# Attention and a two-layer MLP on one core: lower weight parts by subtraction, products kept back at two block changes, the last tile evicted in halves

## The chip, the cores and the metric

The kernel runs on one core of a Trainium2 chip. The engines are TensorE (PE, with its weight loads shown as PEld), VectorE (DVE), ScalarE (ACT), GpSimd (POOL) and SyncE (SP, which here only issues transfers). Matmuls write to PSUM; VectorE and ScalarE read PSUM and write SBUF; transfers (DMA) move data between HBM and SBUF, or within SBUF. The metric is the device time of one execution in microseconds (us), as the median over several runs.

## The reference

Linear attention over 8 batches of 576 tokens (8 heads of 64), then an MLP over all 4608 tokens, in float32:

```python
q_s = softmax(q, axis=-1);  k_s = softmax(k, axis=sequence)
kv = einsum('bhsd,bhse->bhde', k_s, v)
x  = einsum('bhsd,bhde->bhse', q_s, kv)        # as rows: 4608 x 512
h  = x @ w_in                                   # 512 x 2048
g  = h * clip(h + 3, 0, 6) / 6
out = g @ w_out                                 # 2048 x 512
```

The weights arrive as float64; the kernel gets their raw words and makes float32 values of them on the chip.

## The kernel before

**Accuracy.** A float32 matmul is made of three passes in the type float32r: each factor is split into a high part (a cast, ScalarE) and a low part (value minus high part, VectorE), and high x high, high x low and low x high are added up in PSUM. `split` (L121) does a cast and a subtraction; many lines call it, so L123 (the cast) and L124 (the subtraction) stand for many places, told apart by tile names.

**Blocks.** The 4608 rows are NB = 9 blocks `j` of 512 rows. d_ff is NFC = 16 chunks `f` of 128. For each chunk the first GEMM (`gemm1`, tile `ph`, 12 matmuls of 128x512) makes h, the activation makes `g` with its two parts, and the second GEMM (`gemm2`, 4 tiles `po` of 128x512, one PSUM bank each, 12 matmuls) adds the chunk's product into the block's output. Of a chunk's 12 passes, four use the lower part of w_out. After chunk 15, `store` (L596) evicts the four `po` tiles, times 1/6, into `ob` tiles (tile 0 and 2 by ScalarE at L606, 1 and 3 by VectorE at L604) and sends each by SP's queue (L607). `ob` has two buffers, except in the last block.

**Decoding.** In block 0, `decode(f)` (L136) turns a chunk of w_in and w_out (both sides of `raw`, 128x1024 words) into `v` and then into high and low parts in the tile `w_f`: `wi[f]` for w_in, `wo[f]` for w_out. For chunks 0 to 9 that is a split. For chunks 10 to 15 the low part is made in two steps: ScalarE writes -v, rounded to float32r (L168), and a transfer issued by GpSimd adds v to it in place (L169, 512 KB). `v` has three buffers, shared with other tiles (`m` in L306 and L457, `ts`, `xs`).

**Blocks 2 to 8** use a Strassen-like scheme for two chunks (a pair) at once: `fast_pair` (L498) makes seven products of six matmuls of 128x256 each, into `x`, `y` (tile `ph`) and `z` (tile `pz`); ScalarE and VectorE combine them into `first` and `second`, and from those `g` and its two parts, which are put in the space of wi[12], wi[13] for even pairs and wi[14], wi[15] for odd ones (`places`, L520). The factors from the weights are prepared once for each pair by `fast_weights` (L451): three quarters of the pair's w_in (A11, A12, A22) are stored to HBM as they are (L456), four sums S1 to S4 are formed on VectorE (L459 to L470, in `m` and two `ob` tiles), split into the space of that pair's own w_in, and stored (L473, two stores). `fetch` (L486) brings them back, through a ring of 12 places in wi[6] to wi[11] (L495). The factors from x are made by `x_factors`.

**The order.** Python traces the program, and a planner (a list scheduler that simulates the engines) lays out each engine's and each queue's instructions by readiness, traced order and marked priority; each engine and queue then keeps that order. From block 1 on (`in_order`, L684) TensorE keeps the order as traced. The second GEMM lags: its matmuls wait in the list `pend`, from which they are taken by `fill_one` (a whole chunk) or `fill(n)` (n matmuls). In block 0, up to two chunks are kept back; block 1 starts with `gemm1(1, 0)`, then both of them, and each chunk's second GEMM follows one chunk later. In blocks 2 to 8 `fast_pair` calls `slot(n)` between its products to put in 4, 7, 7 and 6 matmuls of the pair before. `slot` also advances `step`, the attention of the next block (L310), whose loads, softmax and small matmuls run beside the MLP. `fast_weights` of pairs 0 to 6 is called in block 1 after each odd chunk, that of pair 7 in block 2's first pair, in its fourth slot.

Of the kernel before, what the change touches and what calls it, by code (L numbers as in the profile page):

```python
# [10 lines left out]
F32 = mybir.dt.float32  # L11
# [7 lines left out]
P = 128  # L19
# [11 lines left out]
def attention_moe(  # L31
# [89 lines left out]
    def split(hi, lo, src, engine=nc.vector):  # L121

        nc.scalar.copy(hi, src)  # L123
        engine.tensor_sub(lo, src, hi.bitcast(F32))  # L124
# [11 lines left out]
    def decode(f):  # L136

        n = 2 * DM
        pairs = raws.pop(f).rearrange("p (n two) -> p n two", two=2)
        low, high = pairs[:, :, 0], pairs[:, :, 1]
        v = moe.tile([P, n], F32, name="v", bufs=3)
        m = v
        nc.scalar.activation(m, high.bitcast(F32), AF.Abs)
        nc.vector.tensor_scalar(m, m, W_MIN, W_MAX, op0=ALU.max, op1=ALU.min)  # L149
        m = m.bitcast(U32)  # L150
        nc.vector.tensor_scalar(
            m, m, 3, 0x3FFFFFFF, op0=ALU.logical_shift_left, op1=ALU.bitwise_and
        )
        vu = v.bitcast(U32)
        nc.vector.scalar_tensor_tensor(  # L155
            vu, high, 0xC0000000, m, op0=ALU.bitwise_and, op1=ALU.bitwise_or
        )
        nc.scalar.activation(low, low, AF.Copy, scale=2.0**-29)
        nc.vector.tensor_tensor(vu, vu, low, op=ALU.add)  # L159
        parts = place(f, F32R, f"w_{f}").rearrange("p (s i n) -> p s i n", s=2, i=2)  # L160
        vs = v.rearrange("p (s n) -> p s n", s=2)
        if f < 10:
            split(parts[:, :, 0], parts[:, :, 1], vs)
        else:

            hi, lo = parts[:, :, 0], parts[:, :, 1]
            nc.scalar.copy(hi, vs)
            nc.scalar.mul(lo, vs, -1.0)  # L168
            nc.gpsimd.dma_start(lo.bitcast(F32), vs, accum_op=ALU.add)  # L169
        wi[f], wo[f] = parts[:, 0], parts[:, 1]  # L170

    FAST = 2
# [277 lines left out]

    def fast_weights(pair):  # L451

        a, b = wi[2 * pair], wi[2 * pair + 1]
        kept[pair] = d = dr.tile([P, 7, 2, HT], F32, name=f"wf{pair}")
        for n, src in ((A11, a[:, :, 0:HT]), (A12, a[:, :, HT:]), (A22, b[:, :, HT:])):
            nc.sync.dma_start(d[:, n], src.bitcast(F32))  # L456
        whole = moe.tile([P, 2 * DM], F32, name="m", tag="v", bufs=3)  # L457
        for at, src in ((0, a), (TB, b)):
            nc.vector.tensor_add(  # L459
                whole[:, at : at + TB], src[:, 0].bitcast(F32), src[:, 1].bitcast(F32)  # L460
            )
        a11, a12, a21, a22 = (whole[:, n * HT : (n + 1) * HT] for n in range(4))
        hi, lo = (t.rearrange("p e n -> p (e n)") for t in (a, b))
        s12, s34 = (moe.tile([P, DM], F32, name="ob", bufs=2) for _ in range(2))
        s1, s2, s3, s4 = (t[:, n : n + HT] for t in (s12, s34) for n in (0, HT))
        nc.vector.tensor_add(s1, a21, a22)
        nc.vector.tensor_sub(s2, s1, a11)
        split(hi[:, 0:TB], lo[:, 0:TB], s12)
        nc.vector.tensor_sub(s3, a11, a21)
        nc.vector.tensor_sub(s4, a12, s2)  # L470
        split(hi[:, TB:], lo[:, TB:], s34)
        for e, t in enumerate((hi, lo)):
            nc.sync.dma_start(  # L473
                d[:, S1 : S4 + 1, e], t.bitcast(F32).rearrange("p (k n) -> p k n", k=4)
            )
# [22 lines left out]
    def fast_pair(j, pair, fill):  # L498

        to = factors(j)  # L500
        x = ps_h.tile([P, TB], F32, name="ph", tag="ph")[:, 0:HT]
        y = ps_h.tile([P, TB], F32, name="ph", tag="ph")[:, 0:HT]
        z = ps_a.tile([P, TB], F32, name="pz", tag="pa")[:, 0:HT]
        seen = set()

        def product(n, ps, name):
            w_hi, w_lo = (come[j, pair, n][:, e] for e in (0, 1))
            f_hi, f_lo = (to[ORDER[n][1]][:, e] for e in (0, 1))
            for i in range(2):
                c = slice(i * P, (i + 1) * P)  # L510
                for k, (w, f) in enumerate(((w_hi, f_hi), (w_hi, f_lo), (w_lo, f_hi))):
                    first = name not in seen
                    seen.add(name)
                    mm(ps, w[:, c], f[:, i], first, i == 1 and k == 2, True)
            del come[j, pair, n]
            fetch(1)

        first = moe.tile([P, TB], F32, name="first", tag="g_hi", bufs=3)
        second = moe.tile([P, TB], F32, name="second", tag="g_lo", bufs=3)
        places = [wi[12 + 2 * (pair % 2) + n] for n in (0, 1)]  # L520
        product(0, z, "z")
        product(1, x, "x")
        with tc.high_priority():
            nc.scalar.copy(first[:, 0:HT], x)
        fill(4)
        product(2, y, "y")
        nc.vector.tensor_add(first[:, 0:HT], first[:, 0:HT], z)
        product(3, x, "x")
        with tc.high_priority():
            nc.scalar.copy(second[:, 0:HT], x)  # L530
        fill(7)
        product(4, x, "x")
        with tc.high_priority():
            nc.scalar.copy(second[:, HT:], x)  # L534
            nc.vector.tensor_add(second[:, HT:], second[:, HT:], y)  # L535
        fill(7)
        product(5, x, "x")
        r = moe.tile([P, TB], F32, name="g", bufs=2)
        with tc.high_priority():
            nc.scalar.activation(r[:, HT:], x, AF.Relu, bias=three, scale=1.0)  # L540
            nc.vector.scalar_tensor_tensor(  # L541
                r[:, HT:], r[:, HT:], 6.0, x, op0=ALU.min, op1=ALU.mult
            )
        h = first[:, 0:HT]
        nc.scalar.activation(r[:, 0:HT], h, AF.Relu, bias=three, scale=1.0)
        nc.vector.scalar_tensor_tensor(
            r[:, 0:HT], r[:, 0:HT], 6.0, h, op0=ALU.min, op1=ALU.mult
        )
        gs = [(places[0][:, 0], places[0][:, 1])]
        split(*gs[0], r)  # L550
        fill(6)
        product(6, y, "y")
        with tc.high_priority():
            nc.vector.tensor_add(second[:, 0:HT], second[:, 0:HT], y)  # L554
        r = moe.tile([P, TB], F32, name="g", bufs=2)
        nc.scalar.activation(r, second, AF.Relu, bias=three, scale=1.0)  # L556
        nc.vector.scalar_tensor_tensor(r, r, 6.0, second, op0=ALU.min, op1=ALU.mult)  # L557
        gs.append((places[1][:, 0], places[1][:, 1]))
        split(*gs[1], r)
        return gs  # L560
# [35 lines left out]
    def store(j, po):  # L596
        for t in range(NTT):
            if j < NB - 1:
                ob = moe.tile([P, DM], F32, name="ob", bufs=2)
            else:  # L600
                ob = place(t, F32, f"ob{t}")[:, 0:DM]
            with tc.high_priority():
                if t % 2:
                    nc.vector.tensor_scalar_mul(ob, po[t], 1.0 / 6.0)  # L604
                else:
                    nc.scalar.mul(ob, po[t], 1.0 / 6.0)  # L606
            nc.sync.dma_start(out[j * TB + t * P : j * TB + (t + 1) * P, :], ob)  # L607


    nc.scalar.activation(three, three, AF.Exp)  # L610
# [67 lines left out]
    for j in range(FAST):  # L678
        for f in range(NFC):
            if j == 0:  # L680
                if f + AHEAD < NFC:
                    load_w(f + AHEAD)
            elif not in_order:
                in_order.append(True)  # L684
            g = gemm1(j, f)
            if j == 0:
                if f + 2 < NFC:
                    decode(f + 2)
            elif f % 2:
                if f < 15:  # L690
                    fast_weights(f // 2)
                if f >= 7:
                    fetch(1 if f < 15 else 12 - len(come))
            next(step, None)

            while len(pend) > 1 - j:
                fill_one()
            pend.append(work(j, [f], [g]))
    for j in range(FAST, NB):
        for pair in range(NFC // 2):  # L700
            done = [0]

            def slot(n):
                fill(n)
                done[0] += 1
                if done[0] in (2, 4):
                    next(step, None)
                if j == FAST and not pair and done[0] == 4:
                    fast_weights(NFC // 2 - 1)

            gs = fast_pair(j, pair, slot)
            fill()
            pend.append(work(j, [2 * pair, 2 * pair + 1], gs))
# [60 lines left out]
```

## Time and profile before

| what | value |
|---|---|
| time, median of 3 runs | 892.21 us (889.02 to 894.39) |
| the profiled execution's own time | 890.79 us |
| its span, first to last instruction | 888.9 us |
| busy share of the span: PE, PEld, DVE, ACT, POOL | 97%, 83%, 69%, 52%, 15% |
| mean granted TensorE clock | 0.99 |
| block 0's first `gemm1` | 33.27 us |
| block 1's first `gemm1` | 137.23 us |
| block 2's first product | 244.00 us |
| TensorE's last matmuls / last eviction | 881.87 us (12, 3.31 us) / 885.20 us |
| mean HBM rate | 204 GB/s |

Times of the trace are microseconds from the span's start. In the views of groups a row gives line, engine, operation, output and inputs, shapes, count, then busy time and the mean duration of one in ns, then the idle time of the engine just before them and what ended it. In the view of waits a row gives who waited for whom: total in us, times, the longest. In the chain of waits and the timeline a row gives start, length and what ran; a bracket gives the idle time before it and what ended that. Matmuls overlap in these rows, so the length of one (about 0.39 us) is more than its spacing (12 in 2.78 us). SPq is SP's queue of transfers; "to landing" is from issue to the last byte.

### The profile page before, as it was taken

To read this page: it belongs to the slowest core of one execution; us is meant where nothing else is said; L and a number is where in the kernel's file an instruction comes from. 1 tells how busy PE (TensorE), PEld (TensorE's weight loads), DVE (VectorE), ACT (ScalarE), POOL (GpSimd) and SP (SyncE) were. 2 spreads that over 40 slices of the span, in tenths; PEclk is the share of its full clock that TensorE was granted. 3 is DMA by queue.
4 is the path that set the end of the run, shared out by engine and by line. 5 is a ranking of instruction groups with operands and counts; after the bars stand their busy time and mean duration, and the time that the engine had idled before them with its cause. 6 is when DMAs were issued, how large, how long until landed. Compare 5 with 4: busy or idle time off the path is not lost.

```text
span 888.9 us, 15262 instructions
## 1 busy us (share of the span) xinstructions
PE 858.4 (97%) x5380; PEld 739.2 (83%) x5380; DVE 614.6 (69%) x1266; ACT 464.8 (52%) x944; POOL 132.9 (15%) x329
## 2 busy tenths in 40 slices
PE   5799998999999999999999999999999999999998
PEld 3578776787789888888888888888888888889896
DVE  7999867899777766767585757676867565444333
ACT  7998753544445454545454545444554554434333
POOL 5000132021212110202020202021212120100000
PEclk9899999999999999999999999999999999999999
DMA  9992583538487668676777668676755575567541
GB/s 372 413 369 84 125 203 136 180 108 289 161 259 224 219 202 258 216 224 203 228 233 229 209 220 259 200 230 195 256 158 183 161 230 170 167 178 224 170 140 47
DMA packets 98474, 185.19 MB, mean 208 GB/s; under 512 B 9824, under 2 KB 24160, under 8 KB 96352
## 3 DMA queue, kind: packets, MB, share of 16 engines
q1 hardware_dynamic: 96192, 180.03, 62.3%
q0 software_dynamic: 1632, 3.15, 2.0%
q10 hardware_dynamic: 576, 1.05, 0.3%
q8 instruction: 43, 0.70, 0.3%
q14 instruction: 31, 0.25, 0.1%
HBM read 156.93 MB, written 24.12 MB: 204 GB/s over the span
## 4 chain that ended last, share of the span: by engine, by line
PE 83%; DVE 7%; DMA 6%; ACT 2%; issue 1%; POOL 0%; SPq 0%; ACTq 0%; DVEq 0%; POOLq 0%
PE po L91 41%; PE ph L91 33%; PE pz L91 4%; PE px L91 2%; PE pkv L91 2%; DMA w<-v 2%; DMA qt<-in_qf_dram 2%; DVE w L124 1%; DMA out_dram<-ob 1%; DVE v L155 1%; DVE v L149 0%; DMA wf<-w 0%; POOL swap L289 0%; DVE km L267 0%; DVE v L159 0%
## 5 line engine op out<-in xcount | busy, mean ns | idle before, releaser
L91 PE MATMUL po<-w,w 128*128 128x512 f32 x1008 | 260.8, 394 | 0.8 <-ACT w L123 0.8
L91 PEld LDWEIGHTS po<-w,w 128*128 128x128 f32 x1008 | 178.4, 189 | 30.7 <-ACT w L123 1.1
L91 PE MATMUL ph<-x_lo,w 128*128 128x256 f32 (+1 forms) x800 | 152.2, 305 | 2.7 <-DVE x_lo L124 2.3
L91 PEld LDWEIGHTS ph<-w,w 128*128 128x128 f32 x1008 | 133.8, 190 | 11.0 <-DVE second L535 1.4
L91 PE MATMUL ph<-x_hi,w 128*128 128x256 f32 (+1 forms) x592 | 138.4, 338 | 4.4 <-DMA w<-v 3.3
L91 PE MATMUL ph<-w,w 128*128 128x256 f32 x1008 | 140.4, 284 | 1.2 <-DVE second L535 1.2
L91 PEld LDWEIGHTS ph<-x_lo,w 128*128 128x128 f32 x800 | 117.0, 189 | 17.0 <-DVE x_lo L124 2.6
L91 PEld LDWEIGHTS ph<-x_hi,w 128*128 128x128 f32 x592 | 93.3, 191 | 18.8 <-DMA w<-v 3.5
L124 DVE TENSOR_TENSOR w<-g,w 128x512 fp32r<-128x512 f32 x112 | 77.2, 689 | 35.3 <-ACT w L123 35.3
L123 ACT CAST w<-g 128x512 fp32r<-128x512 f32 x112 | 69.4, 619 | 56.7 <-DVE g L541 34.4
L91 PE MATMUL po<-w 128*128 128x512 f32 x336 | 86.7, 394 | 0.1
L91 PEld LDWEIGHTS po<-w 128*128 128x128 f32 x336 | 59.4, 188 | 10.8 <-ACT w L123 0.5
L91 PE MATMUL po<-w,g_hi 128*128 128x512 f32 x256 | 67.4, 401 | 0.9 <-ACT g_hi L123 0.9
L556 ACT ACTIVATE g<-second,three 128x512 f32<-128x512 f32 x56 | 40.5, 724 | 33.9 <-DVE second L554 26.5
L91 PEld LDWEIGHTS po<-w,g_hi 128*128 128x128 f32 x256 | 47.7, 190 | 12.2 <-ACT g_hi L123 1.4
L540 ACT ACTIVATE g<-ph,three 128x256 f32<-128x256 f32 x56 | 26.6, 474 | 57.9 <-PE ph L91 57.9
L541 DVE SCALAR_TENSOR_TENSOR g<-g,ph 128x256 f32<-128x256 f32 x56 | 23.2, 415 | 47.1 <-ACT g L540 47.0
L534 ACT COPY second<-ph 128x256 f32<-128x256 f32 x56 | 20.8, 372 | 63.1 <-PE ph L91 63.1
L557 DVE SCALAR_TENSOR_TENSOR g<-g,second 128x512 f32<-128x512 f32 x56 | 39.0, 697 | 15.3 <-ACT g L556 15.2
L91 PE MATMUL pz<-x_hi,w 128*128 128x256 f32 x336 | 49.5, 283 | 0.0
L535 DVE TENSOR_TENSOR second<-second,ph 128x256 f32<-128x256 f32 x56 | 23.1, 413 | 37.5 <-ACT second L534 37.5
L289 POOL COPY swap<-qr 32x16 f32<-32x16 f32 x112 | 30.6, 273 | 96.4 <-DVE qr L301 92.8
(125 smaller groups left out, 1264.2 us busy)
## 6 DMA issues: line engine op xcount, KB each, us to landing
w<-wf SPq DMA_DIRECT2D x392, 256.0 KB, 3.0
raw<-in_w_dram SPq DMA_DIRECT2D x16, 1024.0 KB, 13.4
out_dram<-ob SPq DMA_DIRECT2D x36, 256.0 KB, 3.3
vt<-in_v_dram SPq DMA_DIRECT2D x28, 325.0 KB, 3.5
wf<-w SPq DMA_DIRECT2D x16, 512.0 KB, 4.7
kt<-in_kT_dram SPq DMA_DIRECT2D x28, 288.0 KB, 3.0
ke<-in_k_dram SPq DMA_DIRECT2D x24, 320.0 KB, 2.9
qt<-in_qf_dram SPq DMA_DIRECT2D x28, 256.0 KB, 3.0
```

The costliest lines, as they stand in the source:

```text
L91: nc.tensor.matmul(out, lhsT, rhs, start=start, stop=stop, skip_group_check=goes_on)
L123: nc.scalar.copy(hi, src)
L124: engine.tensor_sub(lo, src, hi.bitcast(F32))
L155: nc.vector.scalar_tensor_tensor(vu, high, 0xC0000000, m, op0=ALU.bitwise_and, op1=ALU.bitwise_or)
L289: nc.gpsimd.tensor_copy(swap[r : r + QD], stat[o : o + QD])
L534: nc.scalar.copy(second[:, HT:], x)
L535: nc.vector.tensor_add(second[:, HT:], second[:, HT:], y)
L540: nc.scalar.activation(r[:, HT:], x, AF.Relu, bias=three, scale=1.0)
L541: nc.vector.scalar_tensor_tensor(r[:, HT:], r[:, HT:], 6.0, x, op0=ALU.min, op1=ALU.mult)
L556: nc.scalar.activation(r, second, AF.Relu, bias=three, scale=1.0)
L557: nc.vector.scalar_tensor_tensor(r, r, 6.0, second, op0=ALU.min, op1=ALU.mult)
```

## The change

1. `decode`, chunks 10 to 15: the lower part of w_in is now made by a VectorE subtraction (128x512); only that of w_out is still negated by ScalarE and completed by the adding transfer (128x512, 256 KB). Chunks 0 to 9 stay as they were.
2. Block 0 to 1: `fill_one()` runs the second GEMM of chunk 14 of block 0 ahead of block 1's first `gemm1`; chunk 15's stays behind it.
3. Block 1 to 2: at block 1's last chunk, the second GEMM of chunk 14 is kept back too, so 24 matmuls instead of 12 go into block 2's first pair. `fast_pair` calls its fill function with 0 there, which `slot` turns into 4 matmuls ahead of the first product, without advancing the attention.
4. `fast_weights` of pair 7 is called in block 1 after chunk 15, like the other pairs, and writes its sums into wi[12] and wi[13] (pair 6's space), since wi[14] and wi[15] are just in use.
5. The last tile of the last block is evicted in two halves: columns 256 to 511 by VectorE, sent by SP's queue; columns 0 to 255 by ScalarE, sent by ScalarE's queue; neither is marked for priority.

```diff
         vs = v.rearrange("p (s n) -> p s n", s=2)
-        if f < 10:
-            split(parts[:, :, 0], parts[:, :, 1], vs)
+        hi, lo = parts[:, :, 0], parts[:, :, 1]
+        nc.scalar.copy(hi, vs)
+        if f < BY_DMA:
+            nc.vector.tensor_sub(lo, vs, hi.bitcast(F32))
         else:
 
-            hi, lo = parts[:, :, 0], parts[:, :, 1]
-            nc.scalar.copy(hi, vs)
-            nc.scalar.mul(lo, vs, -1.0)
-            nc.gpsimd.dma_start(lo.bitcast(F32), vs, accum_op=ALU.add)
+            nc.vector.tensor_sub(lo[:, 0], vs[:, 0], hi[:, 0].bitcast(F32))
+            nc.scalar.mul(lo[:, 1], vs[:, 1], -1.0)
+            nc.gpsimd.dma_start(lo[:, 1].bitcast(F32), vs[:, 1], accum_op=ALU.add)
         wi[f], wo[f] = parts[:, 0], parts[:, 1]
...
         a11, a12, a21, a22 = (whole[:, n * HT : (n + 1) * HT] for n in range(4))
-        hi, lo = (t.rearrange("p e n -> p (e n)") for t in (a, b))
+        at = 2 * min(pair, NFC // 2 - 2)
+        hi, lo = (wi[at + n].rearrange("p e n -> p (e n)") for n in (0, 1))
...
         places = [wi[12 + 2 * (pair % 2) + n] for n in (0, 1)]
+        if (j, pair) == (FAST, 0):
+            fill(0)
         product(0, z, "z")
...
+            rows = out[j * TB + t * P : j * TB + (t + 1) * P, :]
+            if (j, t) == (NB - 1, NTT - 1):
+
+                a, b = slice(0, DM // 2), slice(DM // 2, DM)
+                nc.vector.tensor_scalar_mul(ob[:, b], po[t][:, b], 1.0 / 6.0)
+                nc.scalar.mul(ob[:, a], po[t][:, a], 1.0 / 6.0)
+                nc.sync.dma_start(rows[:, b], ob[:, b])
+                nc.scalar.dma_start(rows[:, a], ob[:, a])
+                continue
             with tc.high_priority():
...
-            nc.sync.dma_start(out[j * TB + t * P : j * TB + (t + 1) * P, :], ob)
+            nc.sync.dma_start(rows, ob)
...
             elif not in_order:
                 in_order.append(True)
+
+                fill_one()
             g = gemm1(j, f)
...
             elif f % 2:
-                if f < 15:
-                    fast_weights(f // 2)
+                fast_weights(f // 2)
                 if f >= 7:
                     fetch(1 if f < 15 else 12 - len(come))
             next(step, None)
 
-            while len(pend) > 1 - j:
+            while len(pend) > (1 if j == 0 or f == NFC - 1 else 0):
                 fill_one()
...
             def slot(n):
-                fill(n)
+                fill(n or 4)
+                if not n:
+                    return
                 done[0] += 1
                 if done[0] in (2, 4):
                     next(step, None)
-                if j == FAST and not pair and done[0] == 4:
-                    fast_weights(NFC // 2 - 1)
```

## The prediction

> **What bounds the kernel now.** I read the page first, then TensorE's waits from 60 to 260 us, then busy time by stretch (columns: stretch and length; busy time and count of PE, PEld, DVE, ACT, POOL; granted clock, DMA share, GB/s).
>
> ```profile
> span 888.9 us, 15262 instructions
> ...
> PE ph L91 <- DMA w<-v: 3.3, 2, 3.0
> PE ph L91 <- DVE x_lo L124: 2.3, 1, 2.3
> PE ph L91 <- DVE second L535: 1.2, 1, 1.2
> PE ph L91 <- ACT x_hi L123: 0.7, 1, 0.7
> PE po L91 <- ACT g_hi L123: 0.5, 1, 0.5
> PE ph L91 <- ACT second L534: 0.4, 1, 0.4
> ...
> 60.00:95.00 35.00, 35.00 (x172) 28.11 (x172) 33.95 (x50) 30.32 (x67) 1.34 (x1) 1.00 0.42 125
> 95.00:145.00 50.00, 43.80 (x219) 33.72 (x218) 39.57 (x71) 27.99 (x44) 12.79 (x26) 0.97 0.68 170
> 145.00:244.00 99.00, 98.46 (x511) 78.62 (x510) 82.59 (x175) 45.47 (x84) 18.93 (x49) 1.00 0.53 175
> 262.00:878.00 616.00, 614.94 (x4113) 547.91 (x4113) 387.56 (x850) 296.24 (x633) 86.77 (x229) 1.00 0.65 204
> ...
> 113.00:117.00 4.00, 3.88 (x12) 3.14 (x13) 1.55 (x3) 2.12 (x3) 2.87 (x5) 0.71 0.82 223
> 117.00:120.00 3.00, 3.00 (x11) 2.19 (x11) 2.57 (x5) 2.80 (x5) 0.25 (x1) 0.82 0.57 98
> 254.00:258.00 4.00, 4.00 (x20) 3.90 (x21) 3.45 (x9) 1.91 (x4) 1.77 (x5) 0.57 0.81 216
> ```
>
> From 262 to 878 us TensorE has 1 us idle in 616: nothing can be won there but by fewer matmuls, and the change takes none away. What it can win lies between 60 and 260 us: six waits of 8.4 us together, and a slower clock behind two of them, 4 us x (1 - 0.71) + 3 us x (1 - 0.82) = 1.7 us after the first, 4 us x (1 - 0.57) = 1.7 us after the last. (I count lost clock only where a stretch shows it.) The rows also show what a gain must live with: VectorE is 97% busy up to 95 us, 79% to 145 us, 83% to 244 us.
>
> The Trainium skill (TensorE: Matmul & The Clock Gate, "The HAM clock gate") says that the clock falls after at least one idle window of about 3.4 us. By that rule gaps as short as these would cost no clock and the sum below would be 3.4 us smaller; the trace disagrees, with 0.71 and 0.57 after shorter gaps, so the rows are used.
>
> **Lower parts of w_in without a transfer.** Six chunks (10 to 15) are decoded with the transfer.
>
> ```profile
> 106.71 6.36 DMA w<-v
> ...
> 113.12 0.73 PE L91 MATMUL ph<-x_hi,w 128*128 128x512 f32 x2 [2.96 <-DMA w<-v]
> 124.32 2.02 PE L91 MATMUL po<-w,g_hi 128*128 128x512 f32 x8
> 133.66 0.73 PE L91 MATMUL ph<-x_hi,w 128*128 128x512 f32 x2 [0.30 <-DMA w<-v]
> ...
> SPq L456 <- DMA w<-v: 31.5, 6, 7.7
> ...
> L124 DVE TENSOR_TENSOR w<-g,w 128x512 fp32r<-128x512 f32 x112 | 77.2, 689 | 35.3 <-ACT w L123 35.3
> L168 ACT ACTIVATE w<-v 128x1024 fp32r<-128x1024 f32 x6 | 6.4, 1060 | 0.0
> ```
>
> Chunk 12's transfer is issued at 106.71 and lands 6.36 us later; the first GEMM waits 2.96 us for it, and 0.30 us for chunk 15's. Now that lower part comes from one 128x512 VectorE subtraction (0.689 us, the nearest form), done some 1 to 2 us after the cast, so before 109 us. Removed: 2.96 + 0.30 us and the 1.7 us of clock, **-5.0 us**. ScalarE saves half of each 1.06 us negation, 3.2 us in all, which buys nothing by itself. The transfer halves to 256 KB and now gates only w_out: chunk 12's second product runs at 124.32 us, 11 us after even the old landing, so its price is nothing; that cover gone, it would be the old 3 us. SP's queue stood 31.5 us behind those transfers before its L456 stores, with the loads of k and q of the next blocks queued behind it; half of that wait (the stores of A11, A12, A22 take only w_in) goes.
>
> Added: 6 x 0.689 = 4.1 us of VectorE, five of the six after 95 us: 3.4 us. It runs beside TensorE, yet VectorE is what is next late. The stretch from 95 to 145 us would shrink to about 42.2 us (50 - 5.0 - 2.8, the next part) and hold 39.57 + 3.4 = 43.0 us of VectorE. At the 97% packing of the row before it that needs 44.3 us, so 2.1 us of the gain are lost if no VectorE work can slide; some can, since fast_weights of pair 0 and softmax of block 2 already stand in this stretch. Bounds 0 to 2.1; I take **+1.0 us**.
>
> **A product kept back between blocks 0 and 1.**
>
> ```profile
> 133.64 1.29 DVE L459 TENSOR_TENSOR m<-w 128x512 f32<-128x512 f32 x2 [1.99 <-DMA w<-v]
> ...
> 140.92 0.50 PE L91 MATMUL ph<-x_hi,w 128*128 128x512 f32 x1 [0.68 <-ACT x_hi L123]
> 143.69 0.51 PE L91 MATMUL ph<-x_lo,w 128*128 128x512 f32 x1 [2.27 <-DVE x_lo L124]
> ...
> 152.90 2.78 PE po L91 x12
> ```
>
> Block 1's first GEMM starts before its last head's x is split and waits 0.68 + 2.27 us, while 24 matmuls of block 0 stand behind it. fill_one() puts 12 of them in front: 2.78 us of cover. x_lo itself also comes earlier by up to the 1.99 us for which VectorE stood behind a transfer. What the x chain loses by the new subtractions is in the 1.0 us above. Bounds: nothing won (x_lo is later by as much) to 2.95; I take **-2.8 us**.
>
> **Products kept back into block 2, and pair 7 prepared one block earlier.**
>
> ```profile
> 252.56 0.69 DVE L604 TENSOR_SCALAR ob<-po 128x512 f32<-128x512 f32 x1 [1.62 <-DMA out_dram<-ob]
> 253.96 1.17 PE L91 MATMUL ph<-w,w 128*128 128x256 f32 x6 [1.24 <-DVE second L535]
> 255.21 0.62 ACT L123 CAST w<-g 128x512 fp32r<-128x512 f32 x1 [1.97 <-DVE g L541]
> ...
> 232.57 0.37 SPq L473 DMA_DIRECT2D wf<-w  x1
> ...
> 263.14 0.62 SPq L473 DMA_DIRECT2D wf<-w  x1
> ...
> L459 DVE TENSOR_TENSOR m<-w 128x512 f32<-128x512 f32 x16 | 10.2, 672 | 2.0 <-DMA w<-v 2.0
> L124 DVE TENSOR_TENSOR w<-ob,w 128x512 fp32r<-128x512 f32 x16 | 10.5, 683 | 4.1 <-PE ph L91 4.1
> L554 DVE TENSOR_TENSOR second<-second,ph 128x256 f32<-128x256 f32 x56 | 23.3, 416 | 4.7 <-PE ph L91 4.3
> ...
> wf<-w SPq DMA_DIRECT2D x16, 512.0 KB, 4.7
> ```
>
> In the first pair of block 2 VectorE stands 1.62 us behind an output transfer with `second` queued after it, and TensorE waits 0.44 + 1.24 us and then runs at 0.57. Only 12 matmuls of block 1 lie between that pair's products now; with 24 (4, 4, 7, 7 and 2) it has the filling of every later pair, and the row from 262 us shows no waits with that filling. Block 1's eviction also moves behind product 5. I take the whole wait and its clock: 0.44 + 1.24 + 1.7, **-3.4 us**; bounds 0 (the stall stands at the eviction's new place) to 3.4. The 0.5 us wait for g_hi stays.
>
> fast_weights of pair 7 moves as a whole: on VectorE 2 x 0.672 + 4 x 0.416 (another 128x256 sum, L554, stands for L466 to L470) + 2 x 0.683 = 4.4 us, two casts on ScalarE, and five stores on SP. They go out of the crowded first pair into 145 to 244 us, where VectorE has 16.4 us idle: no price. That cover gone it would be up to 4.4 us. Its new scratch is chunks 12 and 13, which pair 6's last store (232.57 us, landing 4.7 us later in the median, 237.3) must have left. The first pair of block 2 then puts its g there (the cast at 255.21 us): 18 us for 1.4 us of splits and a 4.7 us store, so nothing is charged; the late case is a rival below.
>
> **The last tile.**
>
> ```profile
> 885.20 0.69 DVE ob L604
> ...
> L534 ACT COPY second<-ph 128x256 f32<-128x256 f32 x56 | 20.8, 372 | 63.1 <-PE ph L91 63.1
> ...
> DMA to landing us min/median/max: 2.0/2.0/2.1
> ...
> w<-wf SPq DMA_DIRECT2D x392, 256.0 KB, 3.0
> ...
> ke<-in_k_dram SPq DMA_DIRECT2D x24, 320.0 KB, 2.9
> ```
>
> One 0.69 us eviction becomes a VectorE half (L554's 0.416) and a ScalarE half (0.372). Side by side that saves 0.28 us; one after the other it costs 0.10 us. No row shows two engines reading one PSUM tile without a dependence between them; I take **0**. A half's transfer, 128 KB, has no row: by size alone it would land 1.0 us sooner than the tail's 2.0; but loads of 320 KB land as soon as those of 256 (2.9 and 3.0), and 512 KB take 4.7, so between nothing and all I take nothing, nearest the loads; bounds 0 to -1.0.
>
> The Trainium skill (PSUM — Partial Sum Buffer, "PSUM bank collisions raise a hardware error") speaks against the halves: two engines may not touch one bank in the same partitions at once, and the compiler adds a dependency. By that rule the halves run in turn and the sum is 0.10 us worse; no run here shows it yet.
>
> **Sum:** -5.0 + 1.0 - 2.8 - 3.4 + 0 = -10.2 us, against the profiled execution's 890.79 us (888.9 us span): 880.6. That execution lies 1.4 us under the median of 892.21, so I forecast **882.0**.
>
> **Rivals.**
> *Only the transfer's part comes (886.6).* The transfer gives 5.0, less 1.0; the x chain, delayed by the subtractions, keeps the wait between blocks 0 and 1, and half of the 3.4 us stays at the eviction's new place. With 0.1 for halves in turn that is -5.6: 885.2, by the median 886.6. For it: VectorE at 79% with 3.4 us added. Against: 1.99 us of VectorE's own waiting goes.
>
> *VectorE is the bound (890.7, no change).* Its added work, 3.4 us in the one stretch and 4.4 us in the other, lands half on top of its busy time and half in its idle time: +3.9, less the 2.0 us behind w<-v, so block 2 starts 1.9 us later instead of 7.8 us earlier; the first pair still gives 3.4. -1.5 us: 889.3, by the median 890.7. For it: 97% busy up to 95 us. Against: 16.4 us idle in block 1.
>
> *Slower: pair 7's scratch (899.7).* If VectorE reaches pair 7's preparation where it does now, the last store leaves at 263.14 us and lands at 267.8, but the cast at 255.21 us now needs that place: 12.6 us of waiting, with ScalarE's evictions of the next products, and so TensorE, behind it, and 1.7 us of clock; the 3.4 us don't come. -6.8 + 14.3 = +7.5: 898.3, by the median 899.7. It decides once that store lands after about 255 us. Against: it is traced ahead of the pair, with 18 us of room.
>
> *It doesn't do what it says (884.8):* (0,14) is laid out behind block 1's first GEMM after all, and the 2.8 us stay.
>
> **How the numbers follow.** Forecast 0.52 (own range 877 to 886), only the transfer's part 0.20, VectorE 0.15, scratch 0.08, the order 0.05. Low end: every gain at its best, -5.0 - 2.95 - 3.4 - 0.28 - 1.0 = -12.6, 879.6 by the median, less the 3.2 us by which the fastest run shown (889.02) lies under it: 876.4. High end: the VectorE case, 891 rounded up. That leaves out the scratch case and some of the edges. About 0.5% is what a measurement of this kernel can tell from no change (887.75 to 896.67): faster 0.72 (forecast, most of the partial cases), same 0.20, slower 0.08.
>
> **What would show it.** Right: no TensorE wait on w<-v; clock 1.00 from 105 to 140 us; block 1's first GEMM behind 12 po matmuls; no wait on `second` in block 2's first pair; first pz at about 234 us, 10 us earlier than 244. Wrong: a wait of TensorE on VectorE's x_lo, g or g_hi above 1 us between 95 and 245 us (VectorE was the bound); ScalarE's cast w<-g waiting on wf<-w near 250 us (scratch); the two last evictions in turn (the halves).

## The result and the profile after

The changed kernel takes **882.85 us** in the median of six runs (881.72 to 884.05), the kernel before 892.12 us (six runs, 889.02 to 894.39): a ratio of **0.990, interval 0.988 to 0.991**, 9.3 us faster. The forecast was 882.0. The profiled execution took 882.45 us; its span is 880.7 us against 888.9.

TensorE's waits from 60 to 260 us in the changed kernel, then busy time by stretch (the columns are those of the prediction's first fence):

```profile
PE po L91 <- ACT g_hi L123: 1.3, 1, 1.3
PE px L91 <- DVE kv_lo L124: 0.8, 1, 0.8
PE ph L91 <- ACT x_hi L123: 0.7, 1, 0.7
PE ph L91 <- DVE g L548: 0.3, 1, 0.3
PE ph L91 <- DVE x_lo L124: 0.2, 1, 0.2
...
105.00:140.00 35.00, 34.09 (x182) 26.31 (x181) 30.76 (x57) 18.36 (x31) 9.16 (x22) 1.00 0.63 169
145.00:244.00 99.00, 96.91 (x521) 78.05 (x521) 84.85 (x182) 47.53 (x88) 19.47 (x48) 1.00 0.59 193
244.00:262.00 18.00, 17.68 (x126) 15.48 (x125) 15.51 (x37) 9.07 (x19) 4.77 (x18) 1.00 0.76 248
```

No wait on w<-v is left, and the clock stays at 1.00 through both places where it had fallen. The waits sum to 3.3 us instead of 8.4, and the 3.4 us of slow clock are gone: 5.1 + 3.4 = 8.5 us. The clock is not a chance of the two profiles: its mean over an execution was 0.992 to 0.994 in the six executions of the changed kernel, and 0.986 to 0.992 in the 52 of the kernel before that ran beside the experiments, 0.9932 against 0.9893 on average. Over a span of 885 us that is about 3.4 us (an estimate). What is still waited for comes from VectorE, or from ScalarE behind it, except for the 0.68 us on x_hi: there ScalarE's cast follows TensorE's own last matmul for x (`px`).

The same kernel's timeline at the places of the change: the decoding of chunk 12, the two block changes and the end. Line numbers are each kernel's own: L168 is the new subtraction, L169 the negation of w_out's half, L170 the transfer.

```profile
104.99 1.04 ACT L163 CAST w<-v 128x1024 fp32r<-128x1024 f32 x1
105.93 0.63 ACT L169 ACTIVATE w<-v 128x512 fp32r<-128x512 f32 x1
106.19 0.69 DVE L168 TENSOR_TENSOR w<-v,w 128x512 fp32r<-128x512 f32 x1
106.86 0.85 POOL L170 DMA_DIRECT2D w<-v  x1 [8.09 <-ACT w L169]
...
132.13 2.10 PE L91 MATMUL po<-w,g_hi 128*128 128x512 f32 x8
134.07 1.08 PE L91 MATMUL po<-w,g_lo 128*128 128x512 f32 x4
134.99 0.40 PE L91 MATMUL ph<-x_hi,w 128*128 128x512 f32 x1
137.08 0.91 PE L91 MATMUL px<-qT,kv 128*128 128x448 f32 x2
138.67 0.49 PE L91 MATMUL ph<-x_hi,w 128*128 128x512 f32 x1 [0.68 <-ACT x_hi L123]
139.39 0.50 PE L91 MATMUL ph<-x_lo,w 128*128 128x512 f32 x1 [0.23 <-DVE x_lo L124]
...
222.26 0.69 DVE L298 TENSOR_REDUCE qm<-qt 128x16 f32<-128x512 f32 x1 [2.77 <-DMA qt<-in_qf_dram]
229.02 2.13 PE L91 MATMUL po<-w,g_hi 128*128 128x512 f32 x8 [1.32 <-ACT g_hi L123]
236.72 0.87 PE L91 MATMUL pz<-x_hi,w 128*128 128x256 f32 x6
248.32 0.98 PE L91 MATMUL ph<-x_hi,w 128*128 128x256 f32 x6 [0.32 <-DVE g L548]
...
876.53 0.42 DVE L613 TENSOR_SCALAR ob<-po 128x256 f32<-128x256 f32 x1 [0.69 <-PE po L91]
876.99 0.33 SPq L615 DMA_DIRECT2D out_dram<-ob  x1
876.99 0.38 ACT L614 ACTIVATE ob<-po 128x256 f32<-128x256 f32 x1 [0.55 <-DVE ob L613]
877.41 0.35 ACTq L616 DMA_DIRECT2D out_dram<-ob  x1
```

The subtraction ends 0.9 us after the cast; the twelve `po` matmuls stand ahead of block 1's first GEMM at 134.99, and yet that GEMM waits 0.68 + 0.23 us. The first `pz` comes at 236.72, 7.3 us earlier than before; 1.9 us of that (8 matmuls of 0.23 us) are only work put off, since 24 matmuls are kept back instead of 12 and 4 of them stand ahead of it. Ahead of the 1.32 us wait on g_hi, VectorE had stood 2.77 us behind a load of q for the next block. At the end ScalarE's half waits for VectorE's. From the start of the last eviction to the end of the span it is now 880.7 - 876.53 = 4.2 us; before it was 888.9 - 885.20 = 3.7 us.

### The profile page after: what moved, and what is told of

Its sections match the earlier page's. It is cut to its first block, busy times and chain, and to the rows that moved or that the text cites. A ratio compares the mean times of both kernels' runs of the same rounds, so it can differ in the third digit from the quotient of the medians.

```text
span 880.7 us, 15266 instructions
## 1 busy us (share of the span) xinstructions
PE 854.8 (97%) x5380; PEld 736.3 (84%) x5380; DVE 616.5 (70%) x1272; ACT 463.0 (53%) x945; POOL 131.8 (15%) x329
## 4 chain that ended last, share of the span: by engine, by line
PE 88%; DVE 6%; DMA 3%; ACT 2%; issue 1%; POOL 0%; SPq 0%; ACTq 0%; DVEq 0%; POOLq 0%
PE po L91 43%; PE ph L91 35%; PE pz L91 4%; PE px L91 3%; PE pkv L91 3%; DMA qt<-in_qf_dram 1%; DVE v L155 1%; DVE w L165 0%; DVE v L149 0%; DMA wf<-w 0%; DVE w L124 0%; DVE x_lo L124 0%; DMA out_dram<-ob 0%; DVE v L159 0%; DMA kq<-in_kT_dram 0%
## 5 line engine op out<-in xcount | busy, mean ns | idle before, releaser
L91 PEld LDWEIGHTS po<-w,g_hi 128*128 128x128 f32 x256 | 47.1, 188 | 12.5 <-ACT g_hi L123 2.2
```

Of the source, the lines that this page charges most:

```text
L91: nc.tensor.matmul(out, lhsT, rhs, start=start, stop=stop, skip_group_check=goes_on)
```

## The experiments

Runs of one and the same kernel lie up to 6 us apart, so two medians within 2 us of each other are not told apart below; their waits in the profile say more, though each profile is one execution. Ratios are to the kernel before on the same chip; its median there was 892.6 to 893.25 us.

**Decode's part alone.**

```diff
 # in the kernel before
-        if f < 10: split(...)  else: cast, negate 1024 columns, add by a transfer of 512 KB
+        chunks 10 to 15: w_in's lower part by VectorE, w_out's by a transfer of 256 KB, as changed
```

> The kernel before with the change of decode alone (lower parts of w_in by VectorE, of w_out by the adding transfer). Theory: TensorE's waits on w<-v (3.3 us) and the slow clock behind them (1.7 us) go, and the wait between blocks 0 and 1 stays, since nothing covers it: 0.9 us left in the changed kernel plus 2.78 us of cover that is missing here, about 3.7 us. Time 892.1 - 5.0 + 0.75 = 887.9. Rival, x of block 1 was late because VectorE and SP's queue stood behind the transfers: then the wait between the blocks shrinks to under 1 us here too, without any cover, and the time is about 892.1 - 5.0 - 2.0 = 885.1.

884.73 us, ratio 0.990 (0.987 to 0.993), 7.9 us under the kernel before. The rival holds by its time, though not quite by its wait (1.2 us, not under 1): most of the gain is here. The timeline between the blocks, with nothing put in front of block 1's first GEMM:

```profile
134.25 0.91 PE L91 MATMUL px<-qT,kv 128*128 128x448 f32 x2
135.84 0.49 PE L91 MATMUL ph<-x_hi,w 128*128 128x512 f32 x1 [0.68 <-ACT x_hi L123]
136.85 0.50 PE L91 MATMUL ph<-x_lo,w 128*128 128x512 f32 x1 [0.52 <-DVE x_lo L124]
...
243.84 0.97 PE L91 MATMUL ph<-x_lo,w 128*128 128x256 f32 x6 [0.44 <-ACT second L535]
245.76 0.98 PE L91 MATMUL ph<-w,w 128*128 128x256 f32 x6 [0.95 <-DVE second L536]
```

The wait on x falls from 2.95 to 1.2 us without any cover. In block 2's first pair 1.4 us stay. (The profiled execution took 880.41 us, the other three 884.66 to 884.84: this profile is the best case of the kernel.)

**A product ahead of block 1's first GEMM, alone and on top of decode's part.**

```diff
                 in_order.append(True)
+                fill_one()
```

> The kernel before with the product of chunk 14 put ahead of block 1's first GEMM, and nothing else. Theory: 2.78 us of matmuls stand in the 2.95 us gap; the waits on x_hi and x_lo sum to 0.2 us, those on w<-v (3.3 us) stay, time 892.1 - 2.8 = 889.3. Rival, x of block 1 depends on TensorE's place (its last matmuls px come later when a product is put ahead): the wait only moves, sums to 2 us or more, and the time is within 0.8 us of 892.1.

> The kernel before with decode's part and the product of chunk 14 ahead of block 1's first GEMM; block 2's first pair, pair 7 and the tail as before. Theory, the wait between blocks 0 and 1 only moves (1.2 us without the product, 0.9 us with it in the changed kernel): no more than 0.5 us won on the decode part alone, 884.2 to 884.7. Rival, the product covers its wait: 884.7 - 1.2 = 883.5 or less.

Alone: 890.61 us, ratio 0.998 (0.9966 to 0.9995), between theory and rival. With decode's part: 884.8 us, 0.991 (0.989 to 0.993), not told apart from decode's part by itself, as its theory had it. In the profile of the product alone:

```profile
114.54 1.22 PE L91 MATMUL ph<-x_hi,w 128*128 128x512 f32 x2 [2.98 <-DMA w<-v]
...
146.86 0.50 PE L91 MATMUL ph<-x_hi,w 128*128 128x512 f32 x1 [1.05 <-ACT x_hi L123]
147.81 0.50 PE L91 MATMUL ph<-x_lo,w 128*128 128x512 f32 x1 [0.45 <-DVE x_lo L124]
```

2.78 us of matmuls were put in and half of the wait, 1.5 us, is still there: x_lo is used at 147.81 instead of 143.69. (1.4 us of that lateness was there before: chunk 12's GEMM starts at 114.54 instead of 113.12.) So the wait partly moves with the cover, as the rival said. The rows show why: the last `px` matmuls, from which the last x is made, stand inside block 1's first GEMM, so what is put ahead of the GEMM puts them off too. With decode's part alone `px` starts at 134.25 and x_hi is waited for 0.68 us; in the changed kernel, with the product ahead, at 137.08, and the wait is 0.68 us again. On top of decode's part the cover takes only the wait on x_lo from 0.52 to 0.23 us: 0.3 us.

**What is left of the change without decode's part** (both products kept back, pair 7 early, the old transfers, last tile whole).

> The changed kernel with the old transfers of 512 KB for chunks 10 to 15 and the last tile whole: what is left of the change without decode's part, that is both kept-back products and pair 7 prepared early. The decode part alone gave 884.7 (-7.9). Theory of a shared cause (the transfers made x of block 1 and the first pair of block 2 late, so covering the waits and removing their cause win the same time): the waits on w<-v and the clock behind them stay (5.0 us), the covers win part of the other 6.4 us, time 892.4 - 4 = 888.4, and the two parts' gains sum to about 12 us, 2 to 3 more than the 9.3 us of the whole. Rival, what is kept back is worth only what it adds to the decode part (1 to 2 us): 890.5 to 891.5.

888.65 us, ratio 0.995 (0.994 to 0.997): 4.6 us, the theory's time. 7.9 + 4.6 = 12.5 us is more than the whole gives, 10.1 us with the last tile whole as here (below). That overlap of 2.4 us is no larger than what the intervals leave open, so the times alone don't show it. The waits do at one place: between blocks 0 and 1 the wait of 2.95 us falls to 1.2 us with decode's part, to 1.5 us with the rest, and to 0.9 us with both. There both parts work on the same wait.

**Decode's part for some of the chunks.**

```diff
+        elif f < 14:     # first kernel;  f >= 14 in the second
             ... w_in by VectorE, w_out by 256 KB
+        else:
+            ... the old transfer of 512 KB
```

> The kernel before with decode's new form for chunks 10 to 13 only; chunks 14 and 15 keep the old transfer of 512 KB. Theory, decode's gain has two sources: TensorE's own 2.96 us wait for chunk 12 with the slow clock behind it (4.7 us), and the 2.0 us that VectorE stands behind the last transfer (chunk 15's) just ahead of block 1's x. Here only the first goes: no wait on w<-v near 110 us, but 2 us or more on x_hi and x_lo between the blocks and up to 0.5 us on chunk 15's transfer; time 892.4 - 4.7 = 887.7. Rival, the whole gain is TensorE's wait and what follows from it: 884.7 as with all six chunks.

> The kernel before with decode's new form for chunks 14 and 15 only; chunks 10 to 13 keep the old transfer. Theory of two sources: the 2.96 us wait for chunk 12 and the slow clock behind it stay, VectorE's 2.0 us behind w<-v go, and the wait between blocks 0 and 1 falls from 2.95 to about 1.2 us; time 892.4 - 0.3 - 1.75 = 890.3. Rival, x of block 1 is late for another reason: the wait between the blocks stays at 2.5 us or more, 892.

Chunks 10 to 13 alone: 892.6 us, ratio 1.000 (0.998 to 1.002), no gain at all. Chunks 14 and 15 alone: 889.0 us, 0.995 (0.994 to 0.997). Neither time came where the theory or the rival put it; the second kernel's waits are those of the theory. The first one's waits (timeline of TensorE, VectorE's waits from 95 to 150 us, clock):

```profile
136.54 1.22 PE L91 MATMUL ph<-x_hi,w 128*128 128x512 f32 x2 [5.55 <-DMA w<-v]
...
DVE m L462 <- DMA w<-v: 6.2, 1, 6.2
...
136.00:140.00 4.00, 3.46 (x8) 2.79 (x9) 3.41 (x7) 0.62 (x1) 0.76 (x4) 0.50 0.61 187
```

and the second one's:

```profile
113.79 1.22 PE L91 MATMUL ph<-x_hi,w 128*128 128x512 f32 x2 [3.23 <-DMA w<-v]
...
141.12 0.49 PE L91 MATMUL ph<-x_hi,w 128*128 128x512 f32 x1 [0.68 <-ACT x_hi L123]
142.09 0.50 PE L91 MATMUL ph<-x_lo,w 128*128 128x512 f32 x1 [0.48 <-DVE x_lo L124]
```

With the early chunks mended, TensorE runs ahead into chunk 15's transfer and waits 5.55 us there, at half the clock behind it; VectorE, standing behind the same transfer, waits 6.2 us. The wait is 5.25 us longer than before for two reasons: TensorE comes to it 2.4 us earlier (130.99 instead of 133.36), and the transfer lands 2.9 us later (136.5 instead of 133.6), since it is issued at 127.44 instead of 126.28 and takes 9.05 us instead of 7.33. Why it is later is not shown. So part of the 2.96 us at chunk 12 was no loss of its own, but held TensorE back from a later wait. (The wait on x is only 0.9 us here: TensorE itself stood behind that transfer.)

With the late chunks mended the early wait stays, and the wait on x falls to the 1.2 us of decode's whole part. The chain of waits in the kernel before says how the last transfer made x late:

```profile
126.28 7.33 DMA w<-v
...
143.03 0.61 DVE x_lo L124
```

Between these two rows stands VectorE's work in its order, with a few GpSimd copies that it waits for: VectorE stood 1.99 us behind the transfer and came late to x_lo. Since one set of chunks wins nothing, the other some 4 us, and both 7.9, the parts of decode are not additive either.

**Pair 7 late, products kept back all the same.**

```diff
-                fast_weights(f // 2)                 # every pair in block 1
+                if f < 15: fast_weights(f // 2)
+                # pair 7 in block 2's first pair, fourth slot, in its own space, as before
```

> The changed kernel with fast_weights of pair 7 back in block 2's first pair (its fourth slot, its own space), all else as changed. Theory, the cover of 24 products makes the first pair's wait go and pair 7's early preparation costs VectorE time in block 1: TensorE's wait on g_hi near 229 us falls from 1.3 to 0.5 us, the waits in block 2's first pair stay under 0.6 us at clock 1.00, time 882.85 - 0.5 = 882.3. Rival, the first pair's wait went because pair 7's VectorE work left it: waits of 1.5 us or more and a clock under 0.8 come back there, time 882.85 + 3.1 - 0.8 = 885.2.

884.1 us, ratio 0.991 (0.989 to 0.993): not told apart from the whole change, nor theory from rival by the time. The waits speak for the theory in the first pair, where the clock is 1.00. The wait on g_hi fell as the theory said, and others came up in the second and third pairs of block 2:

```profile
227.51 2.13 PE L91 MATMUL po<-w,g_hi 128*128 128x512 f32 x8 [0.56 <-ACT g_hi L123]
246.78 0.99 PE L91 MATMUL ph<-x_hi,w 128*128 128x256 f32 x6 [0.30 <-DVE g L548]
254.46 0.97 PE L91 MATMUL ph<-x_lo,w 128*128 128x256 f32 x6 [0.28 <-ACT second L541]
258.08 0.98 PE L91 MATMUL ph<-w,w 128*128 128x256 f32 x6 [0.40 <-DVE second L542]
270.98 0.98 PE L91 MATMUL ph<-w,w 128*128 128x256 f32 x6 [0.90 <-DVE second L542]
```

So 24 products clear the first pair (0.3 us left, just behind it) wherever pair 7 is prepared. By these two profiles VectorE's 4.4 us for pair 7 cost 0.8 us in block 1 (the wait on g_hi, 1.32 instead of 0.56 us), and 1.6 us in block 2 if left there.

**Without the product ahead of block 1, all else as changed** (last tile whole).

> The changed kernel, last tile whole, without the product of chunk 14 ahead of block 1's first GEMM: decode's part, 24 products in block 2's first pair and pair 7 early. Theory, that pair is where the rest of the gain lies: with decode alone it waits 0.4 + 0.9 us and may be clocked down behind it; here at most 0.7 us in all; time 882.5 to 883.2, that is as the whole change. Rival, keeping back into block 2 adds nothing on top of decode: 884.2 to 885.0.

884.15 us, ratio 0.991 (0.989 to 0.992). Between theory and rival: it cannot be told from decode's part alone (884.73) nor from the whole (882.85). Its profile waits 1.2 us on x, 1.3 on g_hi and 0.8 behind block 2's first pair. What the kept-back products add on top of decode's part stays open; it is 0 to 2 us.

**The last tile whole.**

> The changed kernel with the last tile evicted whole by VectorE and sent by SP's queue, as before. Theory, the halves run one after the other and their two transfers end later: from TensorE's last matmul to the span's end 3.7 us as in the kernel before, against 4.2 us with halves; time 882.85 - 0.5 = 882.4, within what can be told from 882.85 in the median, so the spans decide. Rival, only the eviction's 0.15 us counts and the rest is chance: from the last matmul to the end 4.0 to 4.2 us.

882.55 us, ratio 0.989 (0.987 to 0.991), the best kernel of all, though not told apart from the changed one by its median. The spans decide, for the theory: in the twelve kernels here that evict the last tile whole, the time from the start of its eviction to the span's end is 3.55 to 3.70 us, in the two with halves 4.16 and 4.17. The halves cost 0.5 us. Last rows and span:

```profile
span 879.6 us, 15263 instructions
...
875.92 0.69 DVE L612 TENSOR_SCALAR ob<-po 128x512 f32<-128x512 f32 x1 [0.69 <-PE po L91]
```

**More and less of the subtraction on VectorE** (last tile whole in all three): no transfer at all (six more halves on VectorE); w_in's halves on GpSimd; the transfer from chunk 8 on.

```diff
-    BY_DMA = 10
+    BY_DMA = 16          # no transfer
+    BY_DMA = 8           # from chunk 8 on
-            nc.vector.tensor_sub(lo[:, 0], vs[:, 0], ...)
+            nc.gpsimd.tensor_sub(lo[:, 0], vs[:, 0], ...)    # GpSimd
```

> The changed kernel, last tile whole, with every chunk's lower parts made by VectorE: no adding transfer at all, six more halves of 0.69 us (4.1 us) on VectorE, six halves of 0.63 us less on ScalarE. Theory, VectorE is next late between 86 and 240 us: 2 to 4 us of it show on TensorE (longer waits on x_lo, g_hi, kv_lo), time 884.5 to 886.5. Rival, what the transfer still holds (ScalarE 3.2 us behind w<-v for v's buffer) weighs as much as VectorE's work: within 1 us of 882.55, the same kernel with its transfers.

> The changed kernel, last tile whole, with the lower part of w_in for chunks 10 to 15 subtracted by GpSimd instead of VectorE (4.1 us off VectorE; GpSimd takes 0.74 to 1.2 us for 256 columns, so 1.5 to 2.4 us for each of the six). Theory, VectorE is next late there: the wait between the blocks (0.9 us) and those on g_hi (1.3 us) shrink by 1 us or more together, time 881.5. Rival, GpSimd's slower subtraction delays the lower parts and the transfers issued behind it, or block 1's VectorE load is another one: same as with VectorE within 1 us (882.6), or slower.

> The changed kernel, last tile whole, with decode's new form from chunk 8 on instead of 10: two more halves of w_out by transfer, 1.3 us less on VectorE between 70 and 86 us. Theory, VectorE is next late up to block 1 (4.1 us more of it cost 2.5 us): 0.8 us won on 882.55, so 881.7, with TensorE's wait between the blocks not above 0.9 us. Rival, at that place TensorE has no wait and two more transfers hold v's buffers: 882.5 or later.

No transfer: 885.05 us, ratio 0.991 (0.990 to 0.993). GpSimd: 886.82, 0.993 (0.991 to 0.995). From chunk 8: 885.04, 0.991 (0.990 to 0.993). All three come out later than the 882.55 us of the kernel they differ from, GpSimd's clearly; the others' intervals overlap its own a little. The wait on x in each, with a wait of VectorE shortly before it:

```profile
137.25 0.69 DVE L298 TENSOR_REDUCE qm<-qt 128x16 f32<-128x512 f32 x1 [1.92 <-DMA qt<-in_qf_dram]
141.53 0.50 PE L91 MATMUL ph<-x_hi,w 128*128 128x512 f32 x1 [2.26 <-ACT x_hi L123]
```

without any transfer;

```profile
134.62 0.75 DVE L339 TENSOR_REDUCE km<-kt 128x1 f32<-128x576 f32 x1 [0.83 <-DMA kt<-in_kT_dram]
138.36 0.75 DVE L339 TENSOR_REDUCE km<-kt 128x1 f32<-128x576 f32 x1 [0.80 <-DMA kt<-in_kT_dram]
143.58 0.50 PE L91 MATMUL ph<-x_lo,w 128*128 128x512 f32 x1 [1.73 <-DVE x_lo L124]
```

with GpSimd;

```profile
136.72 0.75 DVE L339 TENSOR_REDUCE km<-kt 128x1 f32<-128x576 f32 x1 [1.84 <-DMA kt<-in_kT_dram]
141.54 0.66 PE L91 MATMUL ph<-x_lo,w 128*128 128x512 f32 x1 [1.52 <-DVE x_lo L124]
...
ACT v L148 <- DMA w<-v: 3.7, 1, 3.7
```

with transfers from chunk 8 (below it, ScalarE's wait for a `v` buffer that a transfer holds; it is 3.2 us in the kernel with the last tile whole).

By their times, the theory holds without any transfer (4.1 us more of VectorE, 2.5 us later), and the rivals hold for the other two. The traces show a step in all three that none of them names: the chain of waits ahead of x runs through a load of k or q for the next block. The load starts only when VectorE has done an earlier instruction, takes 5.57, 2.86 and 4.16 us to land, and VectorE, keeping its order, stands behind it for the time shown before it comes to the last x. In the kernel with the last tile whole VectorE waits for no such load between 110 and 145 us. What made VectorE meet these loads in each kernel is not shown; more work for VectorE can have done so in the first, but hardly in the other two, where it has less. (GpSimd takes 1.29 to 1.99 us for a subtraction of 128x512, VectorE 0.69.) Of the divisions tried, half by VectorE from chunk 10 on had the lowest median.

## Why the prediction was right, and where it was not

*The direction and the size* were right: -10.2 us forecast for the profiled execution, -8.3 measured; -9.3 in the medians. Four of the five signs named for "right" are in the profile: no wait on w<-v, clock 1.00, twelve `po` matmuls in front, no wait on `second` in the first pair. The fifth failed: the first pz came 7.3 us earlier, not 10. Two of the three signs named for "wrong" are there too: a wait above 1 us on VectorE's side (1.32 us on g_hi, 0.54 before), and the two last evictions in turn. Both are prices, 0.8 and 0.5 us, and neither turned the result. By the profiles the sum came out as -5.0 (transfer and clock), -2.0 (x), -3.1 (first pair), +1.6 (g_hi and kv_lo) and +0.5 (last tile), -8.0 us together; the span fell by 8.2.

*Lower parts of w_in: right, but for the wrong share.* The 2.96 + 0.30 us and the 1.7 us of clock went. The step, however, priced the wait at chunk 12 as if it could be removed by itself; the run with chunks 10 to 13 alone shows that it could not (0 us won, 5.55 us at chunk 15 instead, in part because that transfer landed later). What the step missed is what else the transfers held: VectorE behind the last one, and with it x of block 1. Decode's part gave 7.9 us, not 4.0 (-5.0 + 1.0).

*The product ahead of block 1: the step that failed.* "fill_one() puts 12 of them in front: 2.78 us of cover", -2.8 us. The wait did fall by 2.0 us in the changed kernel, but it falls by 1.75 us without the product, and with it on top of decode's part the time is not told apart, while the wait falls by another 0.3 us. The step overlooked that the last `px` matmuls stand inside the GEMM that is put off, so that x comes later with the cover. The prediction had noted that x_lo comes earlier by up to 1.99 us once VectorE doesn't stand behind the transfer, and counted the whole wait to the cover all the same.

*Block 2's first pair: the wait went as predicted* (1.7 us to 0.3, clock 1.00). Whether -3.4 us is due to the kept-back products is not shown: with decode's part alone 1.4 us of the wait stay and the clock stayed at 1.00 in the execution profiled. The -2.8 us were won by decode's part for the most part; that the sum came near all the same is partly luck.

*VectorE's price: mis-sized.* +1.0 us for the subtractions and nothing for pair 7. Measured: pair 7 alone 0.8 us at g_hi (1.32 with it, 0.56 without); its term was put at nothing because VectorE had 16.4 us idle in block 1, but idle time elsewhere does not help where its work stands in order ahead of g. Another 0.8 us came up on kv_lo in this execution, and is absent from the profile of the kernel with the last tile whole. What the subtractions themselves cost is not shown: 0.2 us is left on x_lo, and the run without transfers (2.5 us for 4.1) was late through a load.

*The last tile: outside its bounds.* I took 0, with 0.10 us at worst for the eviction; it costs 0.5 us. The eviction itself takes 877.37 - 876.53 = 0.84 us instead of 0.69; the other 0.3 us lie between the last transfer's issue and the end and are not explained by any row; the half's transfer itself lands 1.9 us after its issue, against 2.0 for the whole tile, so half the bytes bought 0.1 us. The Trainium skill (PSUM — Partial Sum Buffer, "PSUM bank collisions raise a hardware error") had it right: ScalarE's half waits for VectorE's (0.55 us), as by a dependence between two readers of one bank. The two engines' writes into one SBUF tile are not what holds it: at 105.93 and 106.19 us ScalarE and VectorE write two halves of one `w` tile at the same time.

*The rivals.* "Only the transfer's part comes" was nearest to the truth about the cause, though not about the time: most of the gain, 7.9 of 9.3 us, comes with the transfer's part alone. VectorE as the bound shows only as a price. The scratch of pair 7 never mattered: no wait on wf<-w stands before a cast w<-g near 250 us.

## What to carry to other kernels

A wait is worth its length only if nothing later holds the same engine: take away the early one alone and TensorE may just walk into the next transfer of the same kind. Before adding cover to one wait and removing the cause of another, ask whether one engine (here VectorE behind a buffer that a transfer holds) makes both late; then their gains do not add. Ask, too, where the work stands from which the covered operand is made: cover that puts it off as well covers little. And a tile in one PSUM bank was not evicted faster here by two engines.

## What the runs showed of the hardware that was not expected

The granted clock fell behind waits of 1.7 to 3 us, and not always. Rows of the clock (the last three columns are granted clock, DMA share, GB/s): in the kernel before, after 0.44 + 1.24 us of waiting, 0.57 (quoted in the prediction); in the kernel with the product ahead of block 1 alone, after 0.44 + 1.69 us at the same place:

```profile
255.00:259.00 4.00, 3.39 (x24) 3.21 (x25) 4.00 (x11) 2.14 (x5) 2.17 (x5) 1.00 0.77 239
```

The longer wait cost no clock. After waits of about 3 us near 110 us it fell each time (before, product ahead alone, late chunks alone, the rest of the change alone), and after 5.55 us too (0.50). Where it was low can be worked out from the rows, if low means half (0.50 is the lowest row here): the prediction's 0.71 and 0.82 are then 2.3 us up to 117 and 1.1 us from there on, 3.4 us in all, from 114.7 to 118.1 us. The 3.4 us ahead of that hold only 1.9 us of the 2.96 us wait. Likewise the 0.57 is 3.4 us of low clock, and the 3.4 us ahead hold 0.44 + 1.24 us of waiting. So in these two cases, by this estimate, about half of such a stretch idle was enough. The Trainium skill (TensorE: Matmul & The Clock Gate, "The HAM clock gate") says that the window in which the engine's activity is watched runs freely and that a change of the clock comes sooner or later with where in it the first matmul lands. That would fit a fall that depends on where in the window a wait lies. Its figure of at least one idle window of about 3.4 us is more than all waits that cost clock here but the one of 5.55 us.

An adding transfer of half the size is not twice as fast: from issue to landing a median of 4.0 us for 256 KB in the changed kernel, 6.0 us for 512 KB in the kernel before, and 9.05 us for chunk 15's 512 KB in the kernel with the early chunks mended.
